# Four chunks that enter transposed, and a tap product added by DMA, in a fused convolution and MLP kernel

## The chip, the cores and the metric

The kernel runs on one core of one Trainium2 chip. The metric is the time of one execution in microseconds (us); the median of three runs is given. A profile records one more execution: for each engine what it did and when. The engines are named as in the profile: PE (TensorE, matmuls), PEld (its weight loads, which overlap the matmuls), DVE (VectorE), ACT (ScalarE), POOL (GpSimd) and SP (SyncE, which here only issues DMAs). Each engine works through its own list of instructions in order and waits on semaphores for the others. DMAs are issued from SP, ACT and POOL.

## The reference, cut to what matters

Two branches share the normalised input xn and are added to x. All arrays have S = 2048 tokens and D = 448 features; the MLP is F = 1792 wide.

```python
x  = A_q
xn = layernorm(x)                                   # over the 448 features, no scale
k_shift = sum(k_pad[:, t:t+S] * shift_k[:, 3-t] for t in range(4))   # 4 taps, causal
kv = k_shift * v
y  = irfft(rfft(kv, 2*S) * rfft(ssm_k, 2*S))[:S] + kv * ssm_D        # long causal convolution
out = x + xn * y + mish(xn @ w1 + b1) @ w2
```

## The kernel before: tiling, stages and the order of the work

**The MLP is the backbone.** The tokens are cut into 8 chunks of 256, the width F into 7 pairs of 2 x 128, which gives 56 (chunk, pair) steps. Every float32 operand of the MLP is split into a high and a low part in the matmul's type, and three partial products are summed. The first product (`g1_mm`, line 457) has 22 matmuls of 256 columns for a pair, the second (`g2_mm`, lines 482 to 484) 12 of 448 columns, and it runs two pairs behind the first. In between `mish` (line 460) has two activations on ACT (line 465) and the split of the result: a cast on ACT (`ach`, line 74) and a subtraction on DVE (`acl`, line 75).

**A chunk's entry.** The first product needs xn with features on partitions. `ln_load` (line 363) brings q with tokens on partitions; `ln_stats` (line 400) takes mean and variance on DVE, the power on POOL, and the normalisation on POOL (chunks 1 to 6) or DVE; these small pieces go into a list, `drip`, from which `dv()` issues one after each of many DVE operations. `ln_T` (line 421) then turns the chunk in two halves of four 128x128 transposes on PE each (line 407), into PSUM, and `x_split` casts (ACT, line 419) and subtracts (DVE, line 417). The halves of chunk c+1 stand at pairs 5 and 6 of chunk c. From chunk 5 on the splits are put off to the end of the half-step (`turned`, `T_LATE`).

**The convolution is laid into the same order.** It is done with two-stage transforms: `f1_mm` (line 118) for the 8 groups of the filter h and for the 8 groups of kv, the fold of their results (`f1_fold`, line 128: a copy on ACT, an addition and a subtraction on DVE, lines 131 to 134), a trip through DRAM (`f1_out`, issued on ACT), then for eight octants `h2_mm`, `v2_mm`, `prod`, `i1_mm`, another trip through DRAM, and last `i2_mm` and the gate with q. The kv groups need `taps` (line 157) first: for each of four taps u a product of k with the tap's weights, added up, and at last multiplied with v (line 175). Products of even taps read a whole k tile (line 162), those of odd taps two halves (lines 165, 167). One product a group, that of tap 2, is made on POOL by `taps_pool` (line 152) into `PP`; `taps` takes it from there if it is there already. The products live in seven buffers, `x`.

**The order is written out by hand.** There are 116 half-steps, two a pair and four at the end: the even one issues the first product, the odd one `mish` and the second product. `at(s, ...)` puts a function ahead of half-step s's MLP work, `after(s, ...)` behind it; within one half-step they go in the order in which they were registered (h, taps and kv, weights, octants, last stage). Times are set by `H_AT` (half-step of each h group's `f1_mm`), `KV_AT` (of each kv group's), `OCT_AT` and `I2_AT`. For kv group g with `f1_mm` at half-step t and d half-steps since the group before (6 for group 0), the taps stand at t - 2 - d + d u/4 (for group 0 one later), `f1_out` at t + 3. `POOL_H = {20: (0, 2)}` makes group 0's tap 2 product on POOL behind h group 5, which stands at 20. Finished chunks are stored by `g2_evac` (line 486) at the half-step where their evacuation is.

Of the kernel before, what the change touches and what calls it, by code (L numbers as in the profile page):

```python
# [15 lines left out]
NJ = 16  # L16
NF = F // 128
NP = NF // 2
CH = 256
# [18 lines left out]
@with_exitstack  # L38
def tile_kernel(ctx: ExitStack, tc, q, k, v, sk, hT, sD, w1, b1, w2, c_f1, c_g, c_gi, c_i2, out):
    nc = tc.nc  # L40
# [16 lines left out]
    Dkv = dp.tile([NO * 16, 32, D], F32, name="Dkv")  # L57
    E = dp.tile([NJ * 4, 64, D], F32, name="E")

    f1id = cp.tile([128, 2, 128], F32, name="f1id")  # L60
    f1, ident = f1id[:, 0], f1id[:, 1]
# [3 lines left out]
    rstd = cp.tile([128, NJ], F32, name="rstd")  # L65


    w1h = wp.tile([128, 4, F], F32R, name="w1h")
# [49 lines left out]
    def f1_mm(src, g, key):  # L118
        x = src.pop(g)
        PS[key, g] = ps = [pc(), pc()]  # L120
        for b in range(2):
            for h in range(2):
                for jj in range(2):
                    rg = 32 * (2 * b + h)
                    nc.tensor.matmul(ps[h][64 * jj:64 * jj + 64, b, :D], f1[rg:rg + 32, 0:64], x[rg:rg + 32, jj],  # L125
                                     start=True, stop=True, tile_position=(rg, 64 * jj))
# [29 lines left out]

    def taps(g, u):
        if (g, u) in PP:
            o = PP.pop((g, u))
        elif u % 2 == 0:  # L160
            o = xt()
            V.tensor_mul(o, KR[g - u // 2], skb[:, u:u + 1].to_broadcast([128, 2, D]))
        else:
            o = xt()
            V.tensor_mul(o[:, 0], KR[g - (u + 1) // 2][:, 1], skb[:, u])
            dv()
            V.tensor_mul(o[:, 1], KR[g - u // 2][:, 0], skb[:, u])
        dv()
        if u == 0:
            KV[g] = o  # L170
        else:
            V.tensor_add(KV[g], KV[g], o)  # L172
            dv()
        if u == 3:
            V.tensor_mul(KV[g], KV[g], VT.pop(g))
            dv()
# [135 lines left out]
    def gate(c):  # L312
        p = PS.pop(("P", c))
        for jj in range(2):
            j = 2 * c + jj
            r = rstd[:, j:j + 1]
# [43 lines left out]

    XS, XN, turned = {}, {}, []

    def ln_load(c, eng=None):
# [3 lines left out]
        else:  # L367
            for jj in range(2):
                nc.sync.dma_start(Q[c][:, jj], q[:, jj])

    def ln_parts(c):
        st = mp.tile([128, 2, 6], F32, name="bst", bufs=2)
        ve = mp.tile([128, 2], F32, name="ve", bufs=2)
        xn = mp.tile([128, 2, D + 64], F32, name="xn", tag="xn", bufs=1)
        XN[c] = xn
        eng = nc.gpsimd if 0 < c < NCHUNK - 1 else V
# [10 lines left out]
        def power(a, b):  # L387
            nc.gpsimd.tensor_tensor(rstd[:, 2 * c + a:2 * c + b], ve[:, a:b], mhalf[:, a:b], op=ALU.pow)  # L388

        def norm(jj):  # L390
            j = 2 * c + jj
            eng.tensor_scalar(xn[:, jj, :D], Q[c][:, jj], mv[:, j, 0:1], rstd[:, j:j + 1],  # L392
                              op0=ALU.subtract, op1=ALU.mult)
# [6 lines left out]
    def ln_stats(c):  # L400
        stats, aggr, eps, power, norm, tail = ln_parts(c)
        drip.extend([lambda: stats(0), lambda: stats(1), lambda: aggr(0), lambda: aggr(1), lambda: eps(0, 2),
                     lambda: [f(*a) for f, *a in ((power, 0, 2), (norm, 0), (norm, 1), (tail, 0, 2))]])

# [16 lines left out]
    def ln_T(c, jj):  # L421
# [4 lines left out]
        transposes(c, jj, p)  # L426

        def halves():
            for lo in range(2):
                x_split(c, jj, p, lo)  # L430

        turned.append(halves)
        if c < T_LATE:
            turn()

    def turn():
        while turned:
            turned.pop()()

# [46 lines left out]
    def g2_evac(c, jjs=(0, 1)):  # L486
        x = Q[c]
        for jj in jjs:
            V.tensor_add(x[:, jj], P2.pop((c, jj))[:, :D], x[:, jj])
            dv()  # L490
            if late(c):
                nc.sync.dma_start(out[:, 2 * c + jj], x[:, jj])
        if not late(c):
            nc.sync.dma_start(out[:, 2 * c:2 * c + 2], x)

    def mlp_slot(s):
# [3 lines left out]
        if half == 0:  # L500
            if i < n:
                c, p = pairs[i]
                if c + 1 < NCHUNK:
                    if p == 0:
                        ln_load(c + 1)
                    if p == (3 if c in (0, 2, NCHUNK - 2) else 2):
                        ln_stats(c + 1)
                    if c == 0:
                        dv(len(drip))
                    if p == NP - 1:  # L510
                        ln_T(c + 1, 1)
                g1_mm(i)
        else:
            if i < n:
                c, p = pairs[i]
                if p == NP - 2 and c + 1 < NCHUNK:
                    ln_T(c + 1, 0)
# [46 lines left out]
    for o in range(NO):  # L564
        s, d = OCT_AT[0] + OCT_AT[1] * o, OCT_AT[1]
        h = s - 1 if o else H0_AT
        at(h - d if o else h - 2, o_load, AH, Dh, o, "ah")
        at(s - d if o else s - 2, o_load, AV, Dkv, o, "av")
# [26 lines left out]
    wz = cp.tile([128, NJ], F32, name="wz")  # L595
    V.memset(wz, 0.0)
    ve0 = cp.tile([128, 2], F32, name="ve0")
    warm = g2p.tile([128, 512], F32, name="pg2")
    for _ in range(WARM):
        nc.tensor.matmul(warm[0:NJ, 0:WARM_N], wz, wz[:, 0:1].to_broadcast([128, WARM_N]), start=True, stop=True)  # L600

# [35 lines left out]
    for s in range(nslots):  # L637
# [7 lines left out]
        for fn, args in fns:  # L645
            if fn in (h2_out, v2_out, i1_out):
                fn(*args)
        turn()
        for fn, args in fns:
# [6 lines left out]
def _constants():  # L656
# [19 lines left out]
    for kk in range(64):  # L676
# [8 lines left out]
    c = lambda a: np.ascontiguousarray(a, dtype=np.float32)  # L685
    return dict(c_f1=c(np.stack([f1, np.eye(128)], axis=1)), c_g=c(G.reshape(128, 8, 4, 2, 32)), c_gi=c(GI.reshape(128, 8, 2, 2, 64)),
                c_i2=c(i2))
# [27 lines left out]
```

## Time and profile before

| | us |
|---|---|
| median of 3 runs | 368.87 |
| lowest, highest | 368.6, 369.53 |
| the profiled execution's own time | 370.86 |
| its span, first to last instruction | 368.9 |
| transposes on PE (line 407), 64 matmuls, busy | 10.3 |
| DVE busy, of the span | 262.5 |
| normalisation on POOL (line 392), 12 operations, busy | 27.8 |

How to read the profile's lines. A group of instructions has line, engine, operation, out<-in by the program's names, shapes and count; then busy time and the mean ns of one; then how long the engine stood idle just before them, and what ended that. A wait is written "engine tile line <- what ended it: us in all, times, longest". A DMA row has the KB of one and the median us from issue to landing. The chain that ended last is followed back from the last instruction through what released each; its rows have start, length and what. Matmuls are pipelined and overlap, so their busy times add to more than the time they take; distances between starts are the better measure. A stage row of the table by windows has the stage, its length, and for PE, PEld, DVE, ACT and POOL the busy time and the number of instructions, then clock, DMA share and GB/s.

### The profile page before, as it was taken

The page shows a single profiled execution, that of the slowest core. Times are in us where ns is not written, and L with a number is a line of the kernel's source. Part 1 is how long each engine was busy: PE and PEld are TensorE (multiplying, and loading weights), DVE is VectorE, ACT ScalarE, POOL GpSimd, SP SyncE. Part 2 cuts the span into 40 slices and gives each one's busy share as a digit, 9 for nine tenths or more (in the row PEclk, how much of TensorE's full clock was granted, in tenths as well). Part 3 has the DMA queues.
Part 4 walks back from the last instruction along what each step waited for, and adds up shares of the span by engine and source line. Part 5 has one row for each costly group of instructions (what it writes and reads, how often), then busy time and mean ns, then how long its engine had stood idle before and what let it go on. Part 6 is the DMA issues. An engine that isn't in the chain of part 4 may idle for free.

```text
span 368.9 us, 7464 instructions
## 1 busy us (share of the span) xinstructions
PE 360.9 (98%) x3128; PEld 292.6 (79%) x3128; DVE 262.5 (71%) x359; ACT 166.3 (45%) x277; POOL 71.2 (19%) x58
## 2 busy tenths in 40 slices
PE   7998999999999999999999999999999999999995
PEld 2697888978888989889868666666666889889885
DVE  5897858999998888996515657656385752897751
ACT  3757543344241443253254555556655533235450
POOL 2005000920228222611006000060000005102020
PEclk9999999999999999999999999999999999999999
DMA  7998996839496329514675598896694375949655
GB/s 241 346 285 312 358 368 184 256 105 295 105 299 214 89 66 274 170 48 101 225 244 174 194 261 238 282 301 189 209 292 125 95 248 205 419 195 276 116 66 133
DMA packets 32354, 79.35 MB, mean 215 GB/s; under 512 B 2881, under 2 KB 19138, under 8 KB 32322
## 3 DMA queue, kind: packets, MB, share of 16 engines
q1 hardware_dynamic: 20210, 44.09, 35.8%
q10 hardware_dynamic: 9776, 22.88, 22.2%
q0 software_dynamic: 2336, 11.93, 11.3%
q8 instruction: 24, 0.39, 0.4%
q14 instruction: 8, 0.07, 0.1%
HBM read 50.44 MB, written 28.44 MB: 214 GB/s over the span
## 4 chain that ended last, share of the span: by engine, by line
PE 71%; DMA 12%; DVE 9%; POOL 3%; ACT 2%; issue 2%; SPq 0%; ACTq 0%; POOLq 0%; DVEq 0%
PE pg L457 27%; PE pg L482 10%; PE pg L484 9%; PE pg L483 9%; PE pc L208 7%; DMA kr<-in_w_dram 6%; PE pc L251 4%; PE pc L125 2%; PE pc L308 2%; DMA Dh<-st 2%; DVE x L172 2%; PE pg L407 2%; POOL xn L392 2%; DMA Dkv<-st 1%; DMA av<-Dkv 1%
## 5 line engine op out<-in xcount | busy, mean ns | idle before, releaser
L465 ACT ACTIVATE a<-pg,b1t 128x256 f32<-128x256 f32 x112 | 47.1, 472 | 113.0 <-PE pg L457 88.2
L457 PE MATMUL pg<-XH,w1h 128*128 128x256 f32 x448 | 91.3, 285 | 0.9 <-ACT XH L419 0.9
L75 DVE TENSOR_TENSOR acl<-a,ach 128x512 fp32r<-128x512 f32 x56 | 38.8, 693 | 65.0 <-ACT ach L74 64.7
L457 PEld LDWEIGHTS pg<-XH,w1h 128*128 128x128 f32 x448 | 69.6, 188 | 18.9 <-issue 15.7
L482 PE MATMUL pg<-w2h,ach 128*128 128x448 f32 x224 | 83.1, 371 | 0.0
L483 PE MATMUL pg<-w2l,ach 128*128 128x448 f32 x224 | 81.3, 363 | 0.9 <-DVE w2l L75 0.9
L484 PE MATMUL pg<-w2h,acl 128*128 128x448 f32 x224 | 81.4, 363 | 0.0
L457 PE MATMUL pg<-XL,w1h 128*128 128x256 f32 x448 | 69.6, 277 | 0.2 <-DVE XL L417 0.2
L457 PEld LDWEIGHTS pg<-XL,w1h 128*128 128x128 f32 x448 | 59.4, 188 | 0.4 <-DVE XL L417 0.4
L457 PE MATMUL pg<-XH,w1l 128*128 128x256 f32 x336 | 56.8, 277 | 0.0
L482 PEld LDWEIGHTS pg<-w2h,ach 128*128 128x128 f32 x224 | 42.0, 188 | 11.7 <-issue 9.4
L457 PEld LDWEIGHTS pg<-XH,w1l 128*128 128x128 f32 x336 | 46.8, 188 | 0.0
L483 PEld LDWEIGHTS pg<-w2l,ach 128*128 128x128 f32 x224 | 42.1, 188 | 3.6 <-DVE w2l L75 1.2
L484 PEld LDWEIGHTS pg<-w2h,acl 128*128 128x128 f32 x224 | 42.1, 188 | 2.5
L388 POOL TENSOR_TENSOR rstd<-ve,mhalf 128x2 f32<-128x2 f32 (+1 forms) x9 | 8.8, 977 | 156.2 <-DVE ve L385 156.1
L74 ACT CAST ach<-a 128x512 fp32r<-128x512 f32 x56 | 34.7, 620 | 1.8
L155 POOL TENSOR_TENSOR x<-kr,skb 128x896 f32<-128x896 f32 x8 | 17.1, 2133 | 83.6 <-DVE x L154 62.4
L392 POOL TENSOR_SCALAR xn<-qt,mv,rstd 128x448 f32<-128x448 f32 x12 | 27.8, 2320 | 0.6
L172 DVE TENSOR_TENSOR x<-x 128x896 f32<-128x896 f32 x24 | 26.8, 1115 | 1.4 <-POOL x L155 0.9
L131 ACT COPY st<-pc 128x896 f32<-128x896 f32 x16 | 14.5, 906 | 14.5 <-PE pc L125 12.6
L132 DVE TENSOR_TENSOR st<-pc,st 128x896 f32<-128x896 f32 x16 | 17.4, 1088 | 3.6 <-ACT st L131 3.1
L259 ACT COPY qe<-pc 128x896 f32<-128x896 f32 x16 | 13.8, 912 | 11.0 <-PE pc L251 10.8
(70 smaller groups left out, 389.7 us busy)
## 6 DMA issues: line engine op xcount, KB each, us to landing
Dh<-st ACTq DMA_DIRECT2D x16, 448.0 KB, 6.4
Dkv<-st ACTq DMA_DIRECT2D x16, 448.0 KB, 5.1
ah<-Dh SPq DMA_DIRECT2D x8, 896.0 KB, 7.0
av<-Dkv SPq DMA_DIRECT2D x8, 896.0 KB, 6.2
E<-qe ACTq DMA_DIRECT2D x16, 448.0 KB, 5.2
e<-E POOLq DMA_DIRECT2D x8, 896.0 KB, 7.9
kr<-in_k_dram SPq DMA_DIRECT2D x10, 448.0 KB, 6.7
x<-in_v_dram SPq DMA_DIRECT2D x8, 448.0 KB, 5.2
```

The costliest lines, as they stand in the source:

```text
L74: nc.scalar.copy(h, raw)
L75: V.tensor_sub(l, raw, h)
L132: V.tensor_add(st[:, 0], e, st[:, 1])
L155: nc.gpsimd.tensor_mul(o, KR[g - u // 2], skb[:, u:u + 1].to_broadcast([128, 2, D]))
L172: V.tensor_add(KV[g], KV[g], o)
L208: nc.tensor.matmul(p[32 * t:32 * t + 32, r, :D], g[rs, t, c], a[rs, t], start=True, stop=True, tile_position=(64 * r, 32 * t))
L392: eng.tensor_scalar(xn[:, jj, :D], Q[c][:, jj], mv[:, j, 0:1], rstd[:, j:j + 1], op0=ALU.subtract, op1=ALU.mult)
L457: nc.tensor.matmul(ps[:, n], l, r, start=n_ == 0, stop=n_ == len(mm) - 1)
L465: nc.scalar.activation(a[:, n], ps[:, n], AF.Mish, bias=b1t[:, 2 * p + n:2 * p + n + 1])
L482: nc.tensor.matmul(ps, ah[:, n, cs], w2h[:, f], start=f == 0, stop=False)
L483: nc.tensor.matmul(ps, ah[:, n, cs], w2l[:, f], start=False, stop=False)
L484: nc.tensor.matmul(ps, al[:, n, cs], w2h[:, f], start=False, stop=f == NF - 1)
```

## The change

Three things, and what goes with them.

1. Chunks 4 to 7 (`NT = 4`) no longer are turned on PE. The host hands in a second copy of q with features on partitions, `qT`, one tile a chunk. The statistics are taken as before from the untransposed q; mean and reciprocal deviation then go to a DRAM tile, `MR` (`nt_store`, on POOL), and come back as a row of 256 numbers, mean and deviation in turn, repeated over all partitions (`nt_row`, on SP), once for each half of the chunk. `nt_norm` subtracts and multiplies in place on DVE, `nt_split` casts and subtracts as before. The row's tile `idr` also holds the identity that the transposes of chunks 0 to 3 use.
2. The product of tap 1 is added to that of tap 0 by an accumulating DMA, SBUF to SBUF, issued on POOL. Taps 2 and 3 are added on DVE (`PP[g]`), and a fifth step (u = 4) adds the two sums and multiplies with v. The times within a group are now t - 2 - d + d (0, 0, 0.5, 0.75, 1), so tap 1 directly follows tap 0, and the last step stands at t - 2.
3. The h groups 3, 0, 4 and 5 stand one half-step later (9, 13, 17, 21), and `POOL_H` moves with group 5 to 21.

Besides: the store of a finished chunk is put one half-step later, kv's last `f1_out` one earlier, the first load of the octants ahead of its half-step by one; the constants `f1` and identity are loaded apart, the identity first; `T_LATE` goes.

```diff
-H_AT = {2: 4, 3: 8, 0: 12, 4: 16, 5: 20, 6: 26, 7: 32}
+H_AT = {2: 4, 3: 9, 0: 13, 4: 17, 5: 21, 6: 26, 7: 32}
+TAP_AT = (0, 0, 0.5, 0.75, 1)
-POOL_H = {20: (0, 2)}
+POOL_H = {21: (0, 2)}
-T_LATE = 5
+NT = 4
+NT_AT = {"q": -5, "x": -1, "stats": -2, "flush": 0, "row": (4, 8), "norm": (7, 10), "split": (8, 11)}
...
     def taps(g, u):
+        if u == 4:
+            V.tensor_add(KV[g], KV[g], PP.pop(g))
+            dv()
+            V.tensor_mul(KV[g], KV[g], VT.pop(g))
+            return dv()
         if (g, u) in PP:
             o = PP.pop((g, u))
...
         if u == 0:
             KV[g] = o
+        elif u == 1:
+            nc.gpsimd.dma_start(KV[g], o, accum_op=ALU.add)
+        elif u == 2:
+            PP[g] = o
         else:
-            V.tensor_add(KV[g], KV[g], o)
-            dv()
-        if u == 3:
-            V.tensor_mul(KV[g], KV[g], VT.pop(g))
+            V.tensor_add(PP[g], o, PP[g])
             dv()
...
+    def xT_load(c):
+        XN[c] = xn_tile()
+        nc.sync.dma_start(XN[c], qT[c])
+
+    def nt_stats(c):
+        stats, aggr, eps, power, norm, tail = ln_parts(c)
+        drip.extend([lambda: stats(0), lambda: stats(1), lambda: aggr(0), lambda: aggr(1),
+                     lambda: (eps(0, 2), power(0, 2), nt_store(c))])
+
+    def nt_store(c):
+        nc.gpsimd.dma_start(MR[c].rearrange("j (p t) -> p j t", t=2), mv[:, 2 * c:2 * c + 2])
+
+    def nt_row(c, jj):
+        nc.sync.dma_start(idr, MR[c][jj].partition_broadcast(128))
+
+    def nt_norm(c, jj):
+        x = XN[c][:, :, 128 * jj:128 * jj + 128]
+        for t, op in enumerate((ALU.subtract, ALU.mult)):
+            m = idr.rearrange("p (a t) -> p t a", t=2)[:, t:t + 1].to_broadcast([128, 4, 128])
+            V.tensor_tensor(x, x, m, op=op)
+            dv()
+
+    def nt_split(c, jj):
+        if jj == 0:
+            x_tiles(c)
+        x, h, l = (t[:, :, 128 * jj:128 * jj + 128] for t in (XN[c], *XS[c]))
+        nc.scalar.copy(h, x)
+        V.tensor_sub(l, x, h)
+        dv()
...
-                if c + 1 < NCHUNK:
+                if c + 1 < NT:
                     if p == 0:
                         ln_load(c + 1)
...
-        for u in range(4):
-            after(t - (2 if g else 1) - d + d * u / 4, taps, g, u)
+        for u in range(5):
+            after(t - (2 if g else 1) - d + d * TAP_AT[u], taps, g, u)
...
-        at(t + 3, f1_out, Dkv, g, "kv")
+        at(t + (3 if g < NO - 1 else 2), f1_out, Dkv, g, "kv")
...
+    for c in range(NT, NCHUNK):
+        b = 2 * NP * (c - 1)
+        at(b + NT_AT["q"], ln_load, c)
+        at(b + NT_AT["x"], xT_load, c)
+        at(b + NT_AT["stats"], nt_stats, c)
+        at(b + NT_AT["flush"], lambda: dv(len(drip)))
+        for jj in range(2):
+            at(b + NT_AT["row"][jj], nt_row, c, jj)
+            after(b + NT_AT["norm"][jj], nt_norm, c, jj)
+            after(b + NT_AT["split"][jj], nt_split, c, jj)
+
+    for c in range(NCHUNK - LATE):
+        after(2 * (NP * (c + 1) + G2_LAG) + 1, g2_out, c)
...
-    nc.scalar.dma_start(f1id, c_f1)
+    nc.scalar.dma_start(ident, c_id)
...
     h_load(H_HEAD, nc.scalar)
+    nc.scalar.dma_start(f1, c_f1)
```

More of the change, by code (lines that the diff above doesn't have):

```diff
@@ L38, in tile_kernel @@
 @with_exitstack
-def tile_kernel(ctx: ExitStack, tc, q, k, v, sk, hT, sD, w1, b1, w2, c_f1, c_g, c_gi, c_i2, out):
+def tile_kernel(ctx: ExitStack, tc, q, qT, k, v, sk, hT, sD, w1, b1, w2, c_f1, c_id, c_g, c_gi, c_i2, out):
     nc = tc.nc
@@ L58, in tile_kernel @@
     E = dp.tile([NJ * 4, 64, D], F32, name="E")
-    f1id = cp.tile([128, 2, 128], F32, name="f1id")
-    f1, ident = f1id[:, 0], f1id[:, 1]
+    MR = {c: dp.tile([2, CH], F32, name="MR") for c in range(NT, NCHUNK)}
+    f1 = cp.tile([128, 64], F32, name="f1")
+    idr = cp.tile([128, CH], F32, name="idr")
+    ident = idr[:, 0:128]
     mhalf = cp.tile([128, 2], F32, name="mhalf")
@@ L65, in tile_kernel, with rs @@
     rstd = cp.tile([128, NJ], F32, name="rstd")
+    def rs(c):
+        return rstd[:, 2 * c:2 * c + 2] if c < NT else mv[:, 2 * c:2 * c + 2, 1]
     w1h = wp.tile([128, 4, F], F32R, name="w1h")
@@ L358, in w2_split @@
         split(w2h[:, 2 * p:2 * p + 2], w2l[:, 2 * p:2 * p + 2], RW.pop(("2", p)))
-    XS, XN, turned = {}, {}, []
+    XS, XN = {}, {}
     def ln_load(c, eng=None):
@@ L369, in ln_load, with xn_tile @@
                 nc.sync.dma_start(Q[c][:, jj], q[:, jj])
+    def xn_tile():
+        return mp.tile([128, 4, CH], F32, name="xn", bufs=1)
     def ln_parts(c):
@@ L426, in ln_T @@
         transposes(c, jj, p)
[L428 to L438, printed above, removed]
+        for lo in range(2):
+            x_split(c, jj, p, lo)
     AHL, P1, P2 = {}, {}, {}
@@ L492, in g2_evac, with g2_out @@
                 nc.sync.dma_start(out[:, 2 * c + jj], x[:, jj])
-        if not late(c):
-            nc.sync.dma_start(out[:, 2 * c:2 * c + 2], x)
+    def g2_out(c):
+        nc.sync.dma_start(out[:, 2 * c:2 * c + 2], Q[c])
     def mlp_slot(s):
@@ L502, in mlp_slot @@
                 c, p = pairs[i]
-                if c + 1 < NCHUNK:
+                if c + 1 < NT:
                     if p == 0:
                         ln_load(c + 1)
-                    if p == (3 if c in (0, 2, NCHUNK - 2) else 2):
+                    if p == (3 if c in (0, 2) else 2):
                         ln_stats(c + 1)
@@ L515, in mlp_slot @@
                 c, p = pairs[i]
-                if p == NP - 2 and c + 1 < NCHUNK:
+                if p == NP - 2 and c + 1 < NT:
                     ln_T(c + 1, 0)
@@ L566, in tile_kernel @@
         h = s - 1 if o else H0_AT
-        at(h - d if o else h - 2, o_load, AH, Dh, o, "ah")
+        (at if o else after)(h - d if o else h - 3, o_load, AH, Dh, o, "ah")
         at(s - d if o else s - 2, o_load, AV, Dkv, o, "av")
@@ L599, in tile_kernel @@
     for _ in range(WARM):
-        nc.tensor.matmul(warm[0:NJ, 0:WARM_N], wz, wz[:, 0:1].to_broadcast([128, WARM_N]), start=True, stop=True)
+        nc.tensor.matmul(warm[0:8, 0:WARM_N], wz, wz[:, 0:1].to_broadcast([128, WARM_N]), start=True, stop=True)
     nc.scalar.activation(ve0, mhalf, AF.Mish)
@@ L647, in tile_kernel @@
                 fn(*args)
-        turn()
         for fn, args in fns:
```

22 lines of the change are left out of this document (12 added, 10 removed).

## The prediction

> Half-steps are numbered as in the program: even ones issue a pair's first product, odd ones the second product of the pair two before. All times are in us.
>
> **What bounds the kernel now.** I read the busy shares first, then the stage table (columns: span, then busy time and instruction count of PE, PEld, DVE, ACT, POOL, then clock, DMA share, GB/s), then who waited for whom, then the chain that ended last.
>
> ```profile
> PE 360.9 (98%) x3128; PEld 292.6 (79%) x3128; DVE 262.5 (71%) x359; ACT 166.3 (45%) x277; POOL 71.2 (19%) x58
> 58.00:112.00 54.00, 54.00 (x430) 46.90 (x428) 52.07 (x75) 19.49 (x35) 16.03 (x9) 1.00 0.74 219
> 192.00:305.00 113.00, 113.00 (x1228) 80.12 (x1213) 68.51 (x84) 60.68 (x91) 12.35 (x9) 1.00 0.73 220
> PE pg L483 <- DVE w2l L75: 0.9, 1, 0.9
> PE pc L208 <- DMA av<-Dkv: 0.3, 1, 0.3
> PE pg L407 <- POOL xn L396: 0.3, 1, 0.3
> ```
>
> PE is the bound: 98% busy, at clock 1.00, and its waits after the start are single ones of 0.3 to 0.9. So every us of work taken off PE is a us of the span, as long as nothing else becomes late. The second thing to see is the stage from 58 to 112: there DVE is busy 52.07 of 54. That is the stage in which the tap products are made, and the change reorders them there. From 192 to 305 DVE has 44 idle.
>
> **What is removed.** Chunks 4 to 7 lose two batches of four transposes each. In the chain (start, length, what) they stand with their neighbours:
>
> ```profile
> 156.68 0.44 PE pg L407 x4
> 157.12 0.21 PE pg L482
> ...
> 159.53 0.44 PE pg L407 x4
> ...
> 204.89 0.59 PE pg L407 x4
> 205.48 2.51 PE pg L457 x22
> 207.99 1.69 PE pc L251 x32
> 209.67 0.40 PE pg L482
> ...
> 213.95 2.72 PE pg L457 x22
> ...
> 313.01 0.44 PE pg L407 x4
> 313.45 2.59 PE pg L457 x22
> ```
>
> The first two of the eight batches and the last are shown, and the fourth. The four of chunks 4 and 7 take 0.44, and two of them make the first product behind them 2.59 instead of 2.51: 4 x 0.44 + 2 x 0.08 = 1.92. The four of chunks 5 and 6 follow a convolution product and take 0.59 like the one shown, but they hide a change of shape that comes back: without a transpose, a matmul behind the convolution takes 0.40 for 0.21, or a first product 2.72 for 2.51. So they return 4 x 0.59 - 2 x 0.19 - 2 x 0.21 = 1.56. **The sum is 3.48.** A second product without a convolution ahead of it lasts 159.53 - 157.12 = 2.41; both lengths are used below.
>
> **What is added and lies beside other work.** Each of the chunks 4 to 7 adds four DVE operations on 128x512; the nearest row is the acl subtraction below, 0.69, so 2.8 a chunk. The splits stay, from SBUF. Chunk 4's fall in the tap stage, the others mostly behind 192, where DVE has room. For chunks 4 to 6 POOL loses the normalisation. New queue work on SP: four 512 KB loads of the transposed input and eight row loads of 128 KB. The second row of a chunk waits in SP's queue for the first normalisation, and what is queued behind it then (tap inputs in chunk 4, the transform loads in chunks 5 and 6) waits too; but it is issued one half-step after that normalisation and has two until its use, so at 2.4 to 2.5 a half-step about 5, and a convolution product more where one lies between. The nearest row of 128 KB says 5.2 from issue to landing; at 7.8, the slowest small load below, DVE would stand for up to 2.8, and at the lower end for nothing. I take nothing, because only the tap stage has DVE near its limit and only chunk 4 falls into it. The store of the statistics has four half-steps, 10, to land.
>
> ```profile
> L75 DVE TENSOR_TENSOR acl<-a,ach 128x512 fp32r<-128x512 f32 x56 | 38.8, 693 | 65.0 <-ACT ach L74 64.7
> out_dram<-q POOLq DMA_DIRECT2D x5, 448.0 KB, 5.4
> qt<-in_q_dram POOLq DMA_DIRECT2D x1, 448.0 KB, 11.3
> g<-in_c_g_dram SPq DMA_DIRECT2D x8, 128.0 KB, 5.2
> b1t<-in_b_dram SPq DMA_DIRECT2D x1, 7.0 KB, 7.8
> ```
>
> The b1t row is also the nearest one for the statistics, small pieces in a slow transfer; by it they land inside their 10, and at the lower end at once. The Trainium skill, "DMA: Bandwidth & Descriptors", Specifications, has pieces under 512 bytes turned into read-modify-write, which speaks against a store of 8-byte pieces; the slow b1t row agrees, and no run here shows the mechanism.
>
> The stores of finished chunks go one half-step later into SP's queue, past the tap loads planned there, and the loads of q five half-steps earlier; both wait for nothing that is late in PE's order, so I count nothing, and 0.3 either way in the range. h's groups 3 and 0, now at half-steps 9 and 13, put their fold ahead of a w2 split on ACT and DVE: 2.5 for ACT (worked out below), 2.2 and 1.1 on DVE, 5.8 of the 1.0 + 2.6 + 2.51 = 6.1 until its use. That is hidden with 0.3 to spare; each 0.1 beyond it is a wait of PE.
>
> **The accumulating DMA.** It takes one 128x896 addition a group off DVE (1.0 when undisturbed, the first L172 row below). Group 0 gives that back: the POOL product of its third tap is now made at half-step 21, while it is asked for at 20, so DVE makes that product itself and the one from POOL is never used. Its landing time isn't in the trace for an SBUF target. The nearest row is the accumulating store, same size, same queue: 5.4. The far end is 11.3, the slowest POOL load of that size; the lower end is nothing, a wait can't be negative. I take 5.4. It hides behind the five half-steps, over 12, between a group's second tap and its last step. The Trainium skill, "DMA: Bandwidth & Descriptors", Anatomy of one DMA — SWDGE (gpsimd) path, gives about 2.0 us plus bytes/436e3; an estimate by it is 3.1 for these 448 KB, and the sum would be the same. The trace's 5.4 for the store differs from it.
>
> **What becomes late.** This decides the sum. Group 0's product for the convolution (L175) must be done when PE comes to half-step 24. The two ACT groups on the way (line, shapes, count, busy, mean ns), the chain up to there, and from the order of time the product itself and PE at half-step 24:
>
> ```profile
> L465 ACT ACTIVATE a<-pg,b1t 128x256 f32<-128x256 f32 x112 | 47.1, 472 | 113.0 <-PE pg L457 88.2
> L74 ACT CAST ach<-a 128x512 fp32r<-128x512 f32 x56 | 34.7, 620 | 1.8
> ```
>
> ```profile
> 63.02 1.02 PE pc L125 x16
> 64.07 0.92 ACT st L131
> 65.01 1.09 DVE st L132
> 66.18 1.05 DVE st L134
> 67.23 1.00 DVE x L172
> 68.25 1.03 DVE acl L75
> 69.27 0.53 DVE x L165
> 69.81 0.55 DVE x L167
> 70.38 1.51 DVE x L172
> ```
>
> ```profile
> 71.91 1.09 DVE L175 TENSOR_TENSOR x<-x 128x896 f32<-128x896 f32 x1
> 73.92 1.01 PE L125 MATMUL pc<-x,f1id 32*64 32x448 f32 x16
> ```
>
> The fold of h's group 5 (L132, L134) starts 2.0 behind its matmuls at half-step 20; the product is done at 73.00, and PE wants it at 73.92: 0.92 to spare. After the change, count from the start T of half-step 21. (a) h's matmuls come there, and ACT first runs that step's two activations and cast, then the copy: 2 x 0.47 + 0.62 + 0.92 = 2.5. (b) DVE from there, by distances of starts: fold 67.23 - 65.01 = 2.2; fourth tap and its addition 0.53 + 0.57 + 1.1 = 2.2; then, ahead of group 0's last step in DVE's order, the first two taps of group 1, 1.0 (as L172 of that size) + 1.1 = 2.1; one acl 0.69; then the last addition and the product with v, 1.0 + 1.1 = 2.1. Together 9.3, so T + 11.8. (c) PE gets to half-step 24 at T + 1.0 + 2.6 + 2.51 + 2.41 = T + 8.5. **PE waits 3.3**, where it waited for nothing. DVE's saved addition doesn't help, because the chain starts at the fold, which is a half-step later than before, with two tap products put between. Group 2 has the same shape around half-step 32 on an even step: fold from 2.0 to 4.2, addition and product to 6.3, PE there at 1.0 + 2.72 + 2.41 = 6.1, about 0.2. The others have their last step in an odd half-step, behind that step's activations, cast and acl: 0.94 + 0.62 + 0.69 + 2.1 and 0.2 of hand-overs = 4.55 of 2.41 + 2.51 = 4.92, so 0.35 to spare.
>
> What may come back: the 0.3 for POOL xn (PE is later, POOL is not), the 0.3 for av (its product is stored a half-step earlier in ACT's order), and some of the 0.9 for w2l, whose neighbours among the loads move: I take 0.1. The smaller first constant load: 0.1.
>
> **The sum:** -3.48 + 3.3 + 0.2 - 0.3 - 0.3 - 0.1 - 0.1 = -0.78. The profiled execution took 370.86 with a span of 368.9, so about 2 lie around the span; the median of the runs is 368.87, as long as that span. I apply the difference to the median: 368.1.
>
> **Rivals.** (1) *No wait at half-step 24.* If DVE's chain is 3 shorter than I count (the fold earlier, or group 0's last step ahead of group 1's taps), the transposes' 3.48 and the 0.6 of the waits are all kept: 368.9 - 4.1 = 364.8. For it: PE is 98% busy and loses work. Against it: the DVE operations counted above, each with its row. (2) *Every group waits a little.* With only 0.35 to spare, DVE operations 0.5 slower in the tap stage cost 0.2 to 0.5 at each of groups 1, 3, 4 and 6, and chunk 4's normalisation, waiting for its row, as much at group 6: about 2 more, 370. For it: L172 at 1.51 beside POOL, 1.00 alone. (3) *The accumulating DMA becomes the bound; slower.* Last step of a group 2.1, two taps of the next 2.1, one acl 0.69, then the landing L, then the last step again: a loop of 4.9 + L. The eight groups' matmuls start from 73.92 to 175.86, 14.56 apart on average, so it decides from L = 9.7. At 11.3 the loop is 16.2, 1.6 x 7 = 11 longer, less about 3 that the first wait and the spare time cover: 368 + 8 = 376. For it: the POOL load of this size at 11.3. Against: it stood behind three others on POOL, and the store that accumulates took 5.4.
>
> ```profile
> 175.86 1.01 PE L125 MATMUL pc<-x,f1id 32*64 32x448 f32 x16
> ```
>
> **How the numbers follow.** A measurement of this kernel can tell about 0.3%, 1.1 us, from no change. The forecast, saving and wait cancel, has 0.52, and its own range is 366.8 to 369.4 (the waits of 0.3 to 0.9 come back or not, the wait of 3.3 by 0.5 either way): 0.22 of it is faster by over 0.3%, 0.30 within. Rival 1 has 0.23, faster. Rival 2 has 0.15, of which 0.05 within and 0.10 slower. Rival 3 has 0.10, slower. Together faster 0.45, within 0.35, slower 0.20. The likeliest is 368.1. For 8 in 10 the range takes in rival 1 to 364.6 and rival 2 to 370.8, and leaves out rival 3.
>
> **What would show it.** L407 with 32 matmuls instead of 64. A PE wait of about 3 ahead of the first L125 that reads a tap product, released by DVE's product with v. Nine DVE tap products from whole k tiles instead of eight, and one POOL product that nobody reads. The accumulating DMA landing in under 7. No PE wait from 192 to 305. I am wrong if that wait is under 1 (then rival 1), if the later groups wait too (rival 2), or if DVE waits for the accumulating DMA for us at a time (rival 3).

## The result

The changed kernel takes 380.37 us (378.32 to 381.14), the kernel before 369.10 on the same chip: a ratio of 1.0287, 95% interval 1.0261 to 1.0313. It is slower by 11, where 368.1 was forecast. The profiled execution of the changed kernel took 380.56 with a span of 378.6. Of the six executions of run 9 below, two ran throughout at a granted clock of 0.85 and 0.56, the profiled one among them, so its ratio is that of the other four, which took 364.68 to 365.35.

The head of the changed kernel's page: the busy time, and the granted clock in 40 slices.

```profile
PE 361.2 (95%) x3096; PEld 293.2 (77%) x3096; DVE 263.6 (70%) x365; ACT 166.3 (44%) x277; POOL 68.0 (18%) x64
PEclk9899999979999999999999999999999999999999
```

PE's busy time didn't fall, 361.2 for 360.9 before, though it does less; and there are slices in which the clock was not at full speed, the second and the ninth. PE's waits, by what ended them (total, times, longest):

```profile
PE pc L132 <- DVE x L161: 4.8, 1, 4.8
PE pg L493 <- ACT XH L465: 2.0, 1, 2.0
PE pc L221 <- ACT ach L81: 1.5, 1, 1.5
PE pc L221 <- DMA av<-Dkv: 1.5, 1, 1.5
PE pg L518 <- DVE qt L525: 1.1, 1, 1.1
```

Before, no wait after the start was longer than 0.9. L161 is a one-element write on DVE directly behind group 0's last product (L168); the wait of 4.8 is the one at half-step 24.

**Where the time went.** The start of each half-step's first MLP matmul was compared in the two traces; the difference, later minus earlier, grows and falls by these amounts (two profiled executions, worked out from PE's order of time):

| half-steps | what the changed kernel loses (+) or gains |
|---|---|
| 0 to 2 (start) | +2.41 |
| 4 to 18 | -1.57 |
| 19 to 23 | +1.57 |
| 24, 25 | +7.28 |
| 34 to 41 | +1.0 |
| 63, 65 | +2.65 |
| 53-55, 67-68, 81-82, 95-97 (transposes) | -3.5 |
| all together, at the last half-step | +10.0 |

The -1.57 says little of the change: kernels below that change nothing there show -1.33 at half-step 10 against the same trace, and that execution of the kernel before took 370.86 against a median of 368.87.

**The wait at half-step 24.** The chain up to it (start, length, what), in the changed kernel:

```profile
62.66 10.61 DMA x<-x
...
73.29 0.63 DVE x L177
73.92 0.55 DVE x L179
...
74.49 1.25 DVE x L188
...
75.82 0.10 DVE x L174
...
76.82 0.65 DVE x L177
77.47 0.54 DVE x L179
78.01 0.60 DVE acl L82
78.61 1.37 DVE x L166
...
80.01 0.07 DVE x L168
...
81.25 1.80 PE pc L132 x16
83.05 4.30 PE pg L493 x22
```

Three things are to be seen. First, the order: group 1's first two taps (75.82 to 78.01) and one acl stand ahead of group 0's last step (L166, L168), as the prediction had it. Second, the first accumulating DMA landed 10.61 after its issue and held the buffer that L177 writes, for 0.7. Third, PE's own work behind the wait: 16 matmuls that take 1.01 took 1.80, and a first product that takes 2.51 took 4.30. The windows show why (columns as in the prediction's stage table: window, span, busy time of PE and the other engines, clock, DMA share, GB/s):

```profile
7.75:11.17 3.42, 1.31 (x9) 1.12 (x10) 2.43 (x5) 2.58 (x5) 0.00 (x0) 1.00 0.96 325
11.17:14.58 3.41, 3.41 (x23) 3.11 (x30) 1.84 (x4) 0.87 (x2) 0.00 (x0) 0.51 0.99 384
...
76.00:79.42 3.42, 0.40 (x2) 0.02 (x1) 3.42 (x5) 0.00 (x0) 3.35 (x3) 1.00 0.95 179
79.42:82.83 3.41, 1.58 (x16) 0.36 (x16) 1.65 (x3) 0.00 (x0) 3.35 (x4) 0.52 0.99 370
82.83:86.24 3.41, 3.41 (x23) 3.27 (x16) 2.13 (x2) 0.91 (x1) 1.39 (x1) 0.50 0.65 123
86.24:89.66 3.42, 3.42 (x24) 3.29 (x24) 0.74 (x2) 1.81 (x4) 0.00 (x0) 0.98 0.48 134
```

In the two windows in which PE idled most (1.31 and 0.40 busy) the clock is still 1.00; in the window behind each it is about half. PE then looks busy for longer with the same matmuls. That is why the busy share doesn't tell of this loss, and the clock column does.

**Half-steps 63 and 65.** The chain there, and the wait of SP's queue at the row load (L434) ahead of it:

```profile
190.42 0.58 ACTq L147
...
191.03 8.20 DMA Dkv<-st
...
199.32 4.75 DMA av<-Dkv
```

```profile
SPq L434 <- DMA MR<-mv: 13.3, 1, 13.3
```

From the changed kernel's list of DMA issues (KB each, median from issue to landing):

```profile
Dkv<-st ACTq DMA_DIRECT2D x16, 448.0 KB, 7.5
av<-Dkv SPq DMA_DIRECT2D x8, 896.0 KB, 7.3
x<-x POOLq DMA_DIRECT2D x8, 448.0 KB, 5.4
```

SP stood 13.3 for the statistics of chunk 5 to land. Behind its row load were queued the first transform loads: ah was issued at 189.04; before it was 177.79, which with PE's lag of 9.8 at that place would be 187.6. The two waits of 1.5 are for them: the one put down to ACT ended when that ah load landed, 6.7 after its issue.

### The profile page after: what moved, and what is told of

Read it like the earlier page. It is cut to its first block, busy times and chain, and to the rows that moved or that the text cites. A ratio compares the mean times of both kernels' runs of the same rounds, so it can differ in the third digit from the quotient of the medians.

```text
span 378.6 us, 7470 instructions
## 1 busy us (share of the span) xinstructions
PE 361.2 (95%) x3096; PEld 293.2 (77%) x3096; DVE 263.6 (70%) x365; ACT 166.3 (44%) x277; POOL 68.0 (18%) x64
## 4 chain that ended last, share of the span: by engine, by line
PE 75%; DMA 10%; issue 8%; DVE 3%; ACT 1%; ACTq 0%; POOLq 0%; DVEq 0%; SPq 0%
PE pg L493 31%; PE pg L518 10%; PE pg L520 9%; PE pg L519 9%; PE pc L221 7%; DMA x<-x 5%; PE pc L264 4%; PE pc L132 4%; DMA Dkv<-st 2%; DMA kr<-in_w_dram 2%; PE pc L321 2%; DMA av<-Dkv 1%; DVE x L166 1%; PE pg L453 1%; DVE x L177 1%
## 5 line engine op out<-in xcount | busy, mean ns | idle before, releaser
L493 PEld LDWEIGHTS pg<-XH,w1h 128*128 128x128 f32 x448 | 71.2, 191 | 20.3 <-issue 15.8
L518 PE MATMUL pg<-w2h,ach 128*128 128x448 f32 x224 | 83.5, 373 | 1.1 <-DVE qt L525 1.1
L493 PE MATMUL pg<-XL,w1h 128*128 128x256 f32 x448 | 70.8, 280 | 0.2 <-DVE XL L463 0.2
L493 PEld LDWEIGHTS pg<-XL,w1h 128*128 128x128 f32 x448 | 60.5, 191 | 0.4 <-DVE XL L463 0.4
L493 PE MATMUL pg<-XH,w1l 128*128 128x256 f32 x336 | 57.6, 280 | 0.0
L518 PEld LDWEIGHTS pg<-w2h,ach 128*128 128x128 f32 x224 | 42.0, 187 | 17.1 <-issue 10.8
L493 PEld LDWEIGHTS pg<-XH,w1l 128*128 128x128 f32 x336 | 47.8, 191 | 0.0
L132 PE MATMUL pc<-x,f 32*64 32x448 f32 x256 | 18.0, 592 | 6.1 <-DVE x L161 4.8
L404 POOL TENSOR_TENSOR mv<-ve,mhalf 128x2 f32<-128x2 f32 x4 | 4.7, 1176 | 105.5 <-DVE ve L401 105.5
L184 POOL DMA_DIRECT2D x<-x x8 | 7.3, 915 | 83.2 <-issue 37.7
L162 POOL TENSOR_TENSOR x<-kr,skb 128x896 f32<-128x896 f32 x8 | 18.1, 2266 | 9.4 <-DVE x L161 9.4
```

The costliest lines, as they stand in the source:

```text
L162: nc.gpsimd.tensor_mul(o, KR[g - u // 2], skb[:, u:u + 1].to_broadcast([128, 2, D]))
L493: nc.tensor.matmul(ps[:, n], l, r, start=n_ == 0, stop=n_ == len(mm) - 1)
L518: nc.tensor.matmul(ps, ah[:, n, cs], w2h[:, f], start=f == 0, stop=False)
```

## The experiments

Theories at the outset: the loss is in the *order* of the tap stage (h's fold a half-step later, group 1's taps ahead of group 0's last step) and in the clock behind it; it is the *accumulating DMA*; or it is the *transposed entry* that costs what it saves. Lags are given as in the table above, against the same trace of the kernel before. The kernel before, measured beside each run, took 369.1 to 370.0; a difference between the medians of two runs is uncertain by about as much, and the lags say where it arises.

**1. The new taps alone, on the kernel before.**

```diff
+        elif u == 1:
+            nc.gpsimd.dma_start(KV[g], o, accum_op=ALU.add)
...
+        for u in range(5):
+            after(t - (2 if g else 1) - d + d * TAP_AT[u], taps, g, u)
```

> The kernel before with the new tap steps alone (second product by the accumulating DMA, fifth step behind the next group's first two taps), h's half-steps as before. Theory (order): h's fold comes 2.5 earlier than in the changed kernel, so of its wait of 4.85 at half-step 24 about 2.3 is left, and the clock may hold: 368.9 + 2.3 = 371 (370 to 374, the upper end with a halved clock). Rival (accumulating DMA): its landing sets the end of the last step; the wait stays near 4.85 and the clock halves: 376. Rival (entry): nothing is lost here, 369 or less.

Measured: 374.35, ratio 1.0150 (1.0124 to 1.0177). PE waits 3.0 at half-step 24, and its next window is at half clock:

```profile
73.97:77.37 3.40, 1.48 (x20) 0.80 (x21) 1.74 (x2) 0.37 (x1) 3.08 (x3) 1.00 0.40 106
77.37:80.79 3.42, 3.42 (x19) 3.42 (x18) 0.00 (x0) 0.53 (x1) 0.16 (x1) 0.52 0.95 238
```

The wait is 0.7 over the 2.3 expected, the time just above the range. In this kernel DVE came to group 0's last step without standing for the first accumulating DMA, so the order of DVE made this wait.

**2. The changed kernel with h early again.**

```diff
-H_AT = {2: 4, 3: 9, 0: 13, 4: 17, 5: 21, 6: 26, 7: 32}
+H_AT = {2: 4, 3: 8, 0: 12, 4: 16, 5: 20, 6: 26, 7: 32}
-POOL_H = {21: (0, 2)}
+POOL_H = {20: (0, 2)}
```

> The changed kernel with h's groups 3, 0, 4, 5 and the POOL product at the half-steps of before. Theory (order): the wait at half-step 24 falls by a half-step, from 4.85 to about 2.3, and with it the halved clock (2.6) may go: 380.4 - 2.5 - 2.6 = 375.3 (374 to 378). Rival (accumulating DMA): the first one lands 10.6 after its issue whatever h does, so at most 0.5 is gained: 380. Rival (entry): 380.

Measured: 377.51, ratio 1.0216 (1.0187 to 1.0245). The wait at half-step 24 fell to 2.6, as expected, but 3.6 were lost at half-step 26 instead. DVE's longest wait in this kernel shows how:

```profile
DVE x L161 <- DMA x<-x: 6.7, 1, 6.7
```

The second accumulating DMA stood in POOL's queue behind chunk 2's normalisation (issued at 78.54, its product ready at 73.5), and the buffer of its tap product is the next that DVE needs. So the DMA does cost something, by when it is issued. With h late another buffer comes next, and this wait is not there.

**3. Group 0's last step ahead of group 1's taps**, h late as in the changed kernel.

```diff
-            after(t - (2 if g else 1) - d + d * TAP_AT[u], taps, g, u)
+            after(t - (2 if g else 1) - d + d * (TAP_AT[u] if g or u < 4 else 5 / 6), taps, g, u)
```

> The changed kernel with group 0's last step put ahead of group 1's first two taps (one half-step earlier, at 22); h late as in the changed kernel. Theory (order): DVE saves the two taps and the wait for a tile between them, about 2.8, ahead of the product: the wait at half-step 24 falls to about 2.0 and the clock may hold: 380.4 - 2.8 - 2.6 = 375 (374 to 378). Rival (accumulating DMA): the last step then stands for the landing: 379 or more. Rival (entry): 380.

Measured: 374.24, ratio 1.0153 (1.0109 to 1.0196): 6.1 less than the changed kernel. In the profiled execution the wait is 1.7, the clock stays at 1.00 through the whole span, and nothing is lost at half-step 25. This one line is about half of the loss (6.1 of 11.3 by the medians, 1.3% of 2.9% by the ratios).

**4. The second tap product added by DVE, in the changed order.**

```diff
         elif u == 1:
-            nc.gpsimd.dma_start(KV[g], o, accum_op=ALU.add)
+            V.tensor_add(KV[g], KV[g], o)
+            dv()
```

> The changed kernel with the second tap product added by DVE again, at the place where the accumulating DMA was issued; order and half-steps as changed. Theory (order): the wait at half-step 24 stays, 4.85 plus 1.0 for the addition of group 1 minus 0.7 for the tile that the DMA held: about 5.1, and the halved clock with it: 380.5 (379.5 to 383). Rival (accumulating DMA): the wait hangs on the slow landing of the first DMA and on the tile that it holds: the wait falls under 3 and the clock drops for one window or none: 376 or less.

Measured: 378.90, ratio 1.0265 (1.0218 to 1.0311), 1.5 less than the changed kernel and just under the range expected; the intervals of the two overlap.

```profile
PE pc L132 <- DVE x L161: 5.1, 1, 5.1
```

The wait is the 5.1 that the order gives. Without any accumulating DMA the loss is nearly whole, so as the bound of the tap stage (rival 3) it falls.

**5. The wait filled with six matmuls** (FILL is 6).

```diff
+        for _ in range(FILL if src is KV and g == 0 else 0):
+            nc.tensor.matmul(ps[0][0:8, 0, :D], wz, wz[:, 0:1].to_broadcast([128, D]), start=True, stop=True)
         for b in range(2):
```

> The changed kernel with six extra matmuls of zeros, 448 columns each (0.75 at full clock by the warm-up ones, 4.5 together), in PE's order ahead of group 0's tap product at half-step 24; they write a PSUM tile that the product then overwrites, so they add no result. They stand in the 4.85 for which PE waits anyway. Theory (clock): PE's idle time there halves its clock for two windows of 3.4, and that costs about 0.9 in the product's own matmuls and 1.6 in the first product behind them; with the wait filled the clock stays at 1.00 and the time falls by 2.5: 380.4 - 2.5 = 377.9, the lag at half-step 24 about 4.9 over the one at 23 and none at 25. Rival (no clock effect of the wait): the halved clock comes anyway, or PE was slow for its operands: 380.4 to 381.

Measured: 377.64, ratio 1.0197 (1.0160 to 1.0235), 2.7 less than the changed kernel, with six matmuls more than it.

```profile
76.70:80.10 3.40, 2.71 (x8) 0.45 (x5) 3.36 (x6) 0.00 (x0) 1.14 (x2) 1.00 0.95 328
80.10:83.52 3.42, 3.37 (x36) 2.67 (x37) 1.28 (x2) 0.91 (x1) 2.10 (x1) 1.00 0.91 222
```

With PE busy for 2.71 of the window the next one stays at 1.00. The lag grew by 5.44 at half-step 24, all of it time until DVE's product was done (DVE stood 0.63 for a tap input and was so much later), and by nothing at 25, where the changed kernel lost 1.57. So it is shown that the wait halves the clock and that the halved clock costs. The size is less sure: these half-steps cost 5.44 for 7.28, 1.84 less, while the time fell by 2.7; the half clock at the start, which this execution lacks, is in the difference too. That the time was expected to 0.2 is in part luck.

**6. The ends of the tap stage as before.**

```diff
-    nc.scalar.dma_start(ident, c_id)
+    nc.scalar.dma_start(f1id[:, 0:192], c_f1)
...
-        at(t + (3 if g < NO - 1 else 2), f1_out, Dkv, g, "kv")
+        at(t + 3, f1_out, Dkv, g, "kv")
...
-        (at if o else after)(h - d if o else h - 3, o_load, AH, Dh, o, "ah")
+        at(h - d if o else h - 2, o_load, AH, Dh, o, "ah")
```

> The changed kernel with the loads at both ends of the tap stage as before: the two constants in one first load, and the first transform loads and the last group's store at their half-steps of before. Taps, h and entry as changed. Theory: the first product starts 0.9 earlier (lag 0 at half-step 0 for 0.88), the early halved clock (1.5) may go with the shorter wait, and the 2.6 of waits at half-steps 63 and 65 go: 380.4 - 0.9 - 2.6 = 376.9, or 375.4 without the early halved clock. Rival: these lags are given back or come from the later PE, not from the loads: 379 or more.

Measured: 378.76, ratio 1.0241 (1.0203 to 1.0279). A miss at half-steps 63 and 65: 2.15 are still lost there for 2.65, so the moved load and store are not what makes them late. At the start it lost 0.55 by half-step 2 instead of 2.41, and most of that is the early half clock, which is missing here. The profiled executions of the five other kernels with the changed one's start (runs 2 to 5 and 11) lacked that half clock too, with first products 0.2 to 0.9 late; so the split load is not shown to be its cause.

**7. The transposed entry alone, on the kernel before**: taps, h, the stores of finished chunks and the transform loads as before.

```diff
+    for c in range(NT, NCHUNK):
+        b = 2 * NP * (c - 1)
+        at(b + NT_AT["q"], ln_load, c)
...
```

> The kernel before with the transposed entry of chunks 4 to 7 alone: taps, h's half-steps, the stores of finished chunks and the loads of the transforms as before, the two constants still in one first load. Theory (taps): everything that the change loses before half-step 53 comes from the new tap steps (their order and the accumulating DMA in POOL's queue) and from h's later groups, and the entry itself brings its 3.5: 368.9 - 3.5 = 365.4 (364.5 to 366.5), with no PE wait over 1 around half-step 24. Rival (entry): its loads, rows and DVE work cost as much as the transposes save: 368 or more. What is left of the gain tells how much the loads added to SP's queue cost around half-step 53.

Measured: 376.31, ratio 1.0159 (1.0123 to 1.0195). (A first form of this kernel, with a constant tile of 16 columns for 8, needed more on-chip memory than there is and has no time.) The first half of the theory holds: up to half-step 54 this kernel is ahead of the kernel before, with no wait at half-step 24. The second half falls: then it loses 1.1 at 55, 1.7 at 60 and 8.1 at 63, and the gain of 3.5 becomes a loss.

```profile
PE pc L215 <- DMA ah<-Dh: 6.5, 1, 6.5
```

In SP's queue a chunk's store waits for its last addition, the row load stands behind the store, and tap inputs and transform loads stand behind the row: ah was issued at 181.73 for 177.79. So there are two losses, one in the taps and one in SP's queue, and the changed kernel contains part of a remedy for the second (the store one half-step later).

**8. The full entry: all of the change but taps, h and the split load.**

```diff
-H_AT = {2: 4, 3: 9, 0: 13, 4: 17, 5: 21, 6: 26, 7: 32}
+H_AT = {2: 4, 3: 8, 0: 12, 4: 16, 5: 20, 6: 26, 7: 32}
...
-            nc.gpsimd.dma_start(KV[g], o, accum_op=ALU.add)
...
-        for u in range(5):
-            after(t - (2 if g else 1) - d + d * TAP_AT[u], taps, g, u)
+        for u in range(4):
+            after(t - (2 if g else 1) - d + d * u / 4, taps, g, u)
...
-    nc.scalar.dma_start(ident, c_id)
+    nc.scalar.dma_start(f1id[:, 0:192], c_f1)
```

> The changed kernel with the taps and h's half-steps of before, and the constants in one first load: the transposed entry with all that came with it (stores of finished chunks a half-step later, the last group's store and the first transform loads moved). Compared with the entry alone, in whose SP queue a store that waits for the chunk's last addition stood ahead of the row and the tap inputs. Theory (queue): the moved store frees the tap inputs at half-step 55, and the moved loads give back most of the 8.1 lost at half-step 63; what stays is the 2.6 that the changed kernel loses at 63 and 65: 368.9 - 3.5 + 2.6 = 368.0 (367 to 370). Rival (taps carry the whole loss, and the entry alone lost only by its clock): 365.4. Rival (entry): no better than alone, 374 or more.

Measured: 371.63, ratio 1.0073 (1.0047 to 1.0100), above the 367 to 370 expected. Nothing is lost before half-step 63, and 4.0 there: PE waits 2.6 for ah, and the next window is at half clock. In front of it SP stood for the statistics, as it does in the changed kernel:

```profile
SPq L428 <- DMA MR<-mv: 15.2, 1, 15.2
```

The profiled execution was the fastest of the six, 368.62. Where the median's other 3 are lost no trace shows.

**9. The same with the statistics earlier**, so that they have landed when the row is asked for.

```diff
-NT_AT = {"q": -5, "x": -1, "stats": -2, "flush": 0, "row": (4, 8), "norm": (7, 10), "split": (8, 11)}
+NT_AT = {"q": -7, "x": -1, "stats": -4, "flush": -3, "row": (4, 8), "norm": (7, 10), "split": (8, 11)}
```

> As the full entry, with the statistics of chunks 4 to 7 two to three half-steps earlier (their q load two, the emptying of their list three), so that their store has landed when SP comes to the first row. Theory (queue): the row no longer holds SP's queue, the first transform load is issued earlier and the waits at 63 and 65 shrink: 1 to 2 below the full entry, 366.5. Rival (the stores and loads share the DMA engines, and the queue does not matter): as the full entry within 0.5.

Measured: 365.28, ratio 0.9880 (0.9859 to 0.9901): faster than both kernels, by about what the transposes save. It gained 6 over the full entry, where 1 to 2 were expected; 4.0 of that is what run 8's trace loses at half-step 63.

**10. The full entry without the store of the statistics.**

```diff
-                     lambda: (eps(0, 2), power(0, 2), nt_store(c))])
+                     lambda: (eps(0, 2), power(0, 2))])
...
-        nc.sync.dma_start(idr, MR[c][jj].partition_broadcast(128))
+        nc.sync.dma_start(idr, qT[c, jj, 0].partition_broadcast(128))
```

> As the full entry, without the store of the statistics; the rows are read from one row of the transposed input instead, same size and same broadcast, so that chunks 4 to 7 are normalised with wrong numbers. Theory (small pieces): the store's 8-byte pieces hold up the stores beside them (packets of 3.5 KB that take 0.26 alone took up to 3.70 behind it), so Dkv's last stores land at 5.4 again instead of 8, the row does not wait, and nothing is lost at 63 and 65: 365.4 to 366. Rival (the row loads and the later loads themselves make the queue late): as the full entry.

Measured: 365.85, ratio 0.9902 (0.9877 to 0.9928). The rows themselves cost nothing; ah is issued at 170.96 for 177.11 in run 8, and nothing is lost at 63. Since run 9 keeps the store and is as fast, it is the wait for its landing that costs, not the store. Why it landed so late can be seen in part. In run 8 it was issued at 167.9, between two stores of Dkv. How long these two took to land in run 8 stands in the first two lines, and in run 10, without the store, in the last two:

```profile
L147 ACTq DMA_DIRECT2D Dkv<-st x2: 592/606/621, 167.8 to 168.4; - x2
DMA to landing us min/median/max: 8.2/8.5/8.9
L147 ACTq DMA_DIRECT2D Dkv<-st x2: 593/607/621, 168.5 to 169.1; - x2
DMA to landing us min/median/max: 4.4/5.1/5.7
```

The store of the statistics itself landed after 8.4 here, and after 3.5 to 3.6 where none of Dkv's went out beside it (at 130.7 in run 8, 141.8 in the changed kernel, 169.3 in run 11). So where they went out together both were late, as the theory had it. That the small pieces are the reason is not shown: the loads on SP also go out at other times in run 10, and the statistics of chunks 6 and 7 landed after 7.0 and 8.4 in the changed kernel, when no store of Dkv was left.

**11. The changed kernel with the earlier statistics of run 9.**

```diff
-NT_AT = {"q": -5, "x": -1, "stats": -2, "flush": 0, "row": (4, 8), "norm": (7, 10), "split": (8, 11)}
+NT_AT = {"q": -7, "x": -1, "stats": -4, "flush": -3, "row": (4, 8), "norm": (7, 10), "split": (8, 11)}
```

> The changed kernel with the statistics of chunks 4 to 7 two to three half-steps earlier, as in the run of the full entry with early statistics; taps and h's half-steps as changed. Theory (two separate losses): the waits at half-steps 63 and 65 (2.65 together) go, because SP no longer stands for the landing of the statistics; the wait at half-step 24 and the start stay: 380.4 - 2.6 = 377.8 (376.5 to 379). Rival (one loss: with the PE late from half-step 24 on, the row's wait costs nothing of its own): 380.4.

Measured: 376.80, ratio 1.0220 (1.0180 to 1.0260), 3.6 less than the changed kernel. ah is issued at 178.03 for 189.04, and no lag grows at half-steps 63 and 65 any more, so this loss is one of its own. The wait at half-step 24 is 5.0 here, and this time only one window is at half clock:

```profile
76.51:79.92 3.41, 0.20 (x8) 0.23 (x16) 3.02 (x4) 0.00 (x0) 3.35 (x3) 1.00 0.98 315
79.92:83.33 3.41, 3.41 (x26) 2.15 (x15) 1.06 (x1) 0.91 (x1) 2.78 (x2) 0.52 0.97 238
```

No run joins this with run 3's order, whose trace still loses 2.3 at half-steps 63 and 65; what the new taps are worth in a better order stays open.

**12. Run 9 with chunk 3 entering transposed as well.**

```diff
-NT = 4
+NT = 3
```

> The full entry with early statistics and the taps of before, with chunk 3 entering transposed as well. Theory (DVE has room in the tap stage once the queue is free): two more batches of transposes go, 0.8 to 1.0: 365.3 - 0.9 = 364.4. Rival (the tap stage is full: DVE was busy 52.07 of 54 there, and chunk 3 adds 2.8 of DVE and two rows to SP's queue ahead of the tap inputs): PE waits for tap products between half-steps 34 and 44: 366 to 370.

Measured: 373.71, ratio 1.0129 (1.0100 to 1.0158); the rival holds, at another place than it named:

```profile
PE pg L487 <- DVE XL L442: 4.4, 1, 4.4
```

PE waits 4.4 for the last split of chunk 3 at half-step 43 and loses 6.4 there with the halved clock. From 119.2 to the start of that split at 130.9 DVE is busy except for 1.7, in which it stands for a tap product of POOL, ahead of which the statistics of chunk 4 ran on POOL (125.6 to 127.8). So most of the wait is that DVE has no room here for a chunk more; those 1.7 come from POOL.

## Why the prediction was wrong

**The transposes were right.** The list of instructions has L453 at 32 matmuls for 64, and the difference of the traces at the four places is 3.5, for 3.48. The four DVE operations a chunk beside them (L440, 16 in all, 11.2) took the 2.8 worked out.

**The wait at half-step 24 was the right mechanism, mis-sized: +3.3 predicted, 7.3 measured.** This is the step that failed first. PE's half was exact: from T (67.86 in this trace) it came to half-step 24 at 76.4, T + 8.5. DVE's chain began at T + 2.5 as worked out, but ended so that PE began at T + 13.4, not T + 11.8: 0.7 for the buffer that the accumulating DMA held, the rest in longer additions (L188 1.25, L166 1.37, for 1.0 to 1.1) beside POOL and in hand-overs. That makes 4.85. The larger miss is the other 2.4: the step "every us of work taken off PE is a us of the span" was used for waits as well, at a clock of 1.00. The kernel before could show nothing else: from the clock's first rise to its last 6 us PE idles at most 0.9 in a window of 3.41. Run 5 takes the clock's part away and leaves the wait; runs 3 and 2 shorten the wait by the order and by h. In the Trainium skill, "TensorE: Matmul & The Clock Gate", Part 1, the clock is gated by activity in free-running windows of 3413 ns. The windows above have that length. Where a wait falls among them fits two half windows in the changed kernel and one in run 11 after nearly equal waits: the wait's end left 1.72 of the next window idle in the one, and nothing in the other. That page of the Trainium skill asks for about one idle window; here PE had still 1.31 (changed kernel) and 1.48 (run 1) of 3.4 busy in a window that was followed by half clock, and the measurement decides.

**The row loads in SP's queue were taken at nothing and cost 2.65.** The prediction named the queue ("what is queued behind it then ... waits too") and dismissed it, because it looked at the second row's wait for the normalisation and at DVE's room. What decided was the first row of chunk 5, at half-step 60: SP stood 13.3 for the statistics, while "they land inside their 10" was counted from their planned half-step. DVE worked them off from 174.99 to 178.5, around the start of half-step 56 (175.7), but SP had come to the row at 174.87 already; POOL stored them at 179.91, beside two stores of Dkv, and they landed 8.3 later, when SP had stood for 13.3. Runs 9, 10 and 11 show it. The prediction also didn't ask what the first transform loads are due for: PE is bound to them at half-step 63. The 0.3 that the sum gives back for av had the wrong sign: PE waits 1.5 for av now. These are PE waits between 192 and 305, where the prediction expected none.

**The start, -0.1 predicted, +2.4 in the profiled execution.** 0.9 are a later first product (w1's half landed at 8.01 for 7.13), 1.5 a window at half clock behind it, which other runs of the same start lack. Why it comes in some is open.

**Half-steps 19 to 23, not priced: +1.6.** Two taps of group 0 and h's fold now stand ahead of chunk 0's last addition on DVE (the wait of 1.1 at L518). The runs with h early don't show it (0.3 in runs 1 and 2), and with one more addition on DVE (run 4) it is 2.5 at half-step 19 for 1.35.

**Rivals.** No wait at half-step 24 at all (364.8) is about what run 9 reaches, with the taps of before. The accumulating DMA as a bound (376) came nearest to the time, and for the wrong reason: run 4 loses nearly as much without it. Its landing, 5.4 in the median, was predicted; the first took 10.61, and what it cost was held buffers. The waits at half-steps 34 to 41, 0.2 predicted for one group, were 1.0 in all.

## What to carry to other kernels

Price a wait on the engine that bounds the kernel at more than its length where that engine's clock follows its activity: here a wait of 4.85 cost 7.3, and with six matmuls of zeros in it the work behind ran at full clock again. When a load that waits for a chain of work is put into a queue, ask what is queued behind it and when that is due, and count the chain from when its first link really runs; moving the statistics two to three half-steps ahead turned a loss of 0.7% into a gain of 1.2%. Adding work to an engine off the critical path is free only if it comes behind what the bound engine waits for next.

## What the runs showed of the hardware

PE's clock changed only at multiples of 3.41 from its first rise, in the traces read here. The table takes PE's idle time in such windows from the order of time of its matmuls, without the last two windows of each run and without run 9 (the windows printed above lie about 0.1 off this grid).

| the window, of 3.41 | idle, followed by half clock | idle, followed by full clock |
|---|---|---|
| at full clock | 3.41 (runs 6 and 7), 3.13 and 2.01 (changed kernel), 3.09 (run 11), 2.52 (run 12), 2.12 (run 4), 1.99 (run 8), 1.81 (run 1), 1.48 (run 2) | 1.88 (run 11), 1.65 and 1.60 (run 7), 1.61, 1.53 and 1.50 (run 2), all of 1.47 and less |
| at half clock | 2.98 (run 4), 1.92 (run 12), 1.72 (changed kernel), 1.42 (run 7), 0.58 (run 6) | 0.59 (run 8), all of 0.02 and less |

So in these runs a window need not be wholly idle: after 1.99 idle or more half clock always followed, between 1.48 and 1.88 it went both ways.
